# Batches 4 to 7: v as the standing operand in two column halves, kv transposed once a batch, z from sums on VectorE

## The chip, the cores and the metric

The kernel runs on one core of a Trainium2 chip. The metric is the device time of one execution in microseconds (us). Before the change the median of three runs is 1175.9 us (1174.65 to 1179.93). The engines have short names here, as in the profile: PE is TensorE (PEld its loads of the standing operand, "weights"), DVE is VectorE, ACT is ScalarE, POOL is GpSimd, SP is SyncE, which here issues DMAs. The suffix q means an engine's sequencer.

## What is computed

Random-feature attention over 8 batches, 8 heads, 576 rows and 64 columns a head, with 128 features, and behind it a gated feed-forward layer on 4608 rows:

```python
def phi(x):
    proj = np.einsum('bhsd,md->bhsm', x, omega)
    sq = np.sum(x * x, axis=-1, keepdims=True) / 2.0
    h = proj - sq
    h = h - np.max(h, axis=-1, keepdims=True)
    return np.exp(h) / np.sqrt(m)
q_p, k_p = (phi(q_s), phi(k_s))
kv = np.einsum('bhsm,bhsd->bhmd', k_p, v)
z = np.sum(k_p, axis=2)
num = np.einsum('bhsm,bhmd->bhsd', q_p, kv)
den = np.einsum('bhsm,bhm->bhs', q_p, z)[..., None] + 1e-06
...
silu = g * (1.0 / (1.0 + np.exp(-g)))
return (silu * val @ w_out).astype(np.float32)
```

`q_s` and `k_s` are q and k scaled; g and val are the attention's output (4608 x 512) times two 512 x 1536 matrices; `w_out` is 1536 x 512.

## The kernel before

The attention runs in 72 steps (`steps`, L124 to L127). Each step has two slots, and a slot is a group of 256 rows of a pair of heads, or the last 64 rows of all four pairs of a batch (a rest group, `None` in `kgroups` and `qgroups`). A batch has 9 groups of k and 9 of q. The first 6 steps (`AHEAD`) hold two k groups each, the next 60 one q group and one k group, the last 6 two q groups. So the k groups of batches 4 to 7 lie in steps 30 to 65, and the q groups of batch 4 begin at step 42.

What a group goes through is spread over several steps. `st_transpose` (L393) turns its rows (`pt`, `x`), `st_project` (L412) multiplies them with omega (`pp`; the two heads of a pair lie in two halves of the array's rows), `st_max` (L431) finds maxima on DVE, `st_exp` (L451) makes the features `ph` on ACT. For k, `k_accumulate` (L543) follows two steps later (`KLAG`): the features `ph` stand in the array (128 x 128), and v with a column of ones, 65 columns, moves. So kv comes out with features as rows, and z as its 65th column. The accumulator `kvacc` holds two pairs of heads (`a2` is 0 or 1); when it is complete, `kv_finalize` (L472) copies it to `kvr`.

For q there are two ways. Batches 0 to 3 (`b < BPOOL`) are multiplied with kv and z at once (`q_mult`, L589), divided on DVE, and turned in `q_out` by a transpose (L635). For batches 4 to 7 the denominator is made ahead: `q_den` (L504) multiplies the features with z on POOL, which needs z in all 128 partitions (`zt`), and sums on DVE (`dj`); `q_norm` scales the features, `q_transpose` turns them (`ptq`, L585, copied to `qt`), and `q_out` (L627) multiplies with kv standing, one head in each half of the array's columns (`xt`, L642). To spread z, `kv_finalize` turns it on PE (`zp`, L481), ACT copies it (`zs`), a DMA writes it to DRAM (`zd`), and at the step of the batch's first q group `load_z` reads it back into all partitions.

PSUM is scarce. `ps_att` (tag "b"), `ps_tr` (tag "t") and the accumulators of kv (tag "kv") have one bank each. `ptq` of the first q group of a step lies in `ps_att`, and so do `zp`, and `xt` of a step's second q group.

Between these parts the layer's products run on the same PE: `g` and `v` at L678 and `o` at L687, each of 512 moving columns, later `a`, `c`, `d` at L912. How many of them a step takes is set ahead by a plan of costs (`course`, `give`); the order of the parts within a step is the list `GROUPED` from step 25 on. A scheduler of the framework makes the final order of each engine, and may move an instruction past others of its engine; `issue_after` and `behind_step` (L257) forbid some of that. Each engine executes its instructions in order. Where the output of a group is for tiles 3 to 8 it goes through a copy `xo` (L656) and a DMA to DRAM (`xs`).

At the start q, k and v are loaded by SP, except v of the first step and of the first rest group (`vrest`, four DMAs), which ACT issues (L387).

Of the kernel before, what the change touches and what calls it, by code (L numbers as in the profile page):

```python
# [23 lines left out]
def kernel(  # L24
# [11 lines left out]
    nc = tc.nc  # L36
# [57 lines left out]

    ident = const.tile([P, P], F32, name="ident")
    make_identity(nc, ident)

    def ps_att(name, shape):
        return ps_a.tile(shape, F32, name=name, tag="b")
# [30 lines left out]
    def slots(n, kind):  # L130

        if not 0 <= n < NS:
            return []
        return [(i, b, g, (kgroups if kd == "k" else qgroups)[g]) for i, (kd, b, g) in enumerate(steps[n]) if kd == kind]

    def pairs_of(gr):
        return [(2 * c, 2 * c + 1) for c in range(CH)] if gr is None else [gr[:1]] * CH
# [240 lines left out]
    def load_v(n):  # L378
        for i, b, g, gr in slots(n, "k"):
            rest = gr is None  # L380
            ts = (vtile, vrest)[rest]
            t = ts[nv[rest] % len(ts)]
            nv[rest] += 1
            assert t not in busy, "v's tile is still needed"
            busy.append(t)
            vrows[b, g] = t
            load_group(t, v, b, gr, True, nc.scalar if n == 0 or n < AHEAD and gr is None else nc.sync)  # L387

    box = {}
    sts = {}  # L390


    def st_transpose(n):  # L393
        if n >= NS:
            return
        nat = nats.pop(n)
        pt = ps_tr(f"pt_{n}", [P, 2, G])
        for i in range(2):
            for c in range(CH):
                nc.tensor.transpose(  # L400
                    pt[:, i, c * P : (c + 1) * P], nat[:, i, c].rearrange("p h d -> p (h d)"), ident
                )
        x = att.tile([P, 2, G], F32, name=f"x_{n}", tag="x")

        st = att.tile([P, 4, 2, CH, 2], F32, name=f"st_{n}", tag="st", bufs=6)
        sq = att.tile([P, 2, CH, 2, D], F32, name=f"sq_{n}", tag="sq")
        nc.gpsimd.tensor_tensor(sq, nat, nat, op=ALU.mult)  # L407
        nc.scalar.copy(x, pt)  # L408
        sts[n] = x, st, sq
        return True  # L410

# [60 lines left out]
    def kv_finalize(b, a2):  # L472
        acc = kvacc.pop((b, a2))
        raw = att.tile([P, 4, VW], F32, name=f"kvr{b}_{a2}", tag="kvr", bufs=4)
        nc.scalar.copy(raw, acc)
        for j in range(2):
            kvst[b, 2 * a2 + j] = raw[:, 2 * j : 2 * j + 2, :]
        if b >= BPOOL:

            zp = ps_att(f"zp{b}_{a2}", [4, P])  # L480
            nc.tensor.transpose(zp, raw[:, :, D], ident)  # L481
            zs = att.tile([4, P], F32, name=f"zs{b}_{a2}", tag="zs")
            nc.scalar.copy(zs, zp)
            zd = dram.tile([4, P], F32, name=f"zd{b}_{a2}", tag="zd", bufs=4)
            nc.sync.dma_start(zd, zs)
            zds[b, a2] = zd

    zds = {}
    zbc = {}

    def load_z(n):

        for _, b, g, gr in slots(n, "q"):
            if g == 0 and b >= BPOOL:
                zt = att.tile([P, 2, 4, M], F32, name=f"zt{b}", tag="zt")
                for a2 in range(2):
                    nc.sync.dma_start(
                        zt[:, a2], zds.pop((b, a2)).rearrange("(o h) m -> o h m", o=1).broadcast_to([P, 4, M])
                    )
                    zbc[b, a2] = zt[:, a2]  # L500

    dns = {}

# [39 lines left out]
    def k_accumulate(n, half):  # L543

        n -= KLAG
        ks = [(b, g, gr, c) for _, b, g, gr in slots(n, "k") for c in range(CH)]
        for b, g, gr, c in ks[half * len(ks) // 2 : (half + 1) * len(ks) // 2]:
            ph, vt = box["k", b, g], vrows[b, g]
            if c == CH - 1:
                busy.remove(vt)  # L550
                del box["k", b, g]
            for j, pr in enumerate(pairs_of(gr)[c]):
                a2 = pr // 2
                first = (b, a2) not in kvacc
                if first:
                    kvacc[b, a2] = ps_k.tile([P, 4, VW], F32, name=f"kvacc{b}_{a2}", tag="kv")
                acc = kvacc[b, a2]
                done.setdefault((b, a2), []).append(pr)
                last = LAST[pr] == (g, c)
                for hh in range(2):  # L560
                    nc.tensor.matmul(  # L561
                        acc[:, 2 * (pr % 2) + hh, :],
                        ph[:, c, hh * M : (hh + 1) * M],
                        vt[:, 2 * c + j if gr is None else c, hh, :],
                        start=first and hh == 0,
                        stop=last,
                        skip_group_check=True,
                    )
                if len(done[b, a2]) == NACC:
                    kv_finalize(b, a2)  # L570
        return bool(slots(n, "k"))

    qts = {}
    xns = {}
# [52 lines left out]
    def q_out(n):  # L627
        n -= OLAG
        for i, b, g, gr in slots(n, "q"):
            po = (ps_att if n + OLAG < EARLY or i else ps_tr)(f"xt{b}_{g}", [P, G])  # L630
            first = column(b, gr)
            if b < BPOOL:
                xn = xns.pop((b, g))
                for c in range(CH):
                    nc.tensor.transpose(po[:, c * P : (c + 1) * P], xn[:, c].rearrange("p h d -> p (h d)"), ident)  # L635
            else:
                qt = qts.pop((b, g))

                segs = [(pr, pr * RES, RES) for pr in range(NPAIR)] if gr is None else [(gr[0], 0, G)]
                for pr, o, w in segs:  # L640
                    for hh in range(2):
                        nc.tensor.matmul(  # L642
                            po[hh * D : (hh + 1) * D, o : o + w], kvst[b, pr][:, hh, 0:D], qt[:, hh, o : o + w],
                            start=True, stop=True, skip_group_check=True,
                        )
            j, o = tile_of(first)
            if gr is None:
                parts_ = [(po.rearrange("d (r c) -> d r c", c=RES), slice(0, NPAIR), j, o, RES)]
            else:
                cut = min(TILES[j][1] - o, G)  # L650
                parts_ = [(po[:, 0:cut], gr[0], j, o, cut)]
                if cut < G:
                    parts_.append((po[:, cut:G], gr[0], j + 1, 0, G - cut))
            for src, pr, j, o, w in parts_:
                if j in x_dram:
                    xo = att.tile(list(src.shape), F32, name=f"xo{b}_{g}_{j}", tag="xo", bufs=3)  # L656
                    nc.scalar.copy(xo, src)
                    nc.sync.dma_start(x_dram[j][:, pr, o : o + w], xo)
                    continue
                if j not in xt:  # L660
                    xt[j] = [xres.tile([P, NPAIR, T], F32R, name=f"x{e}{j}", tag=f"x{e}") for e in "hl"]
                hi, lo = (t[:, pr, o : o + w] for t in xt[j])
                nc.scalar.copy(hi, src)
                nc.vector.tensor_tensor(lo, src, hi.bitcast(F32), op=ALU.subtract)
            if gr is None or gr[0] == NPAIR - 1:
                cols_done[0] = first + (RES if gr is None else G)
        return bool(slots(n, "q"))
# [383 lines left out]
    def give(us):  # L1051
# [28 lines left out]
    )  # L1080
    GROUPED = (
        q_out,
        st_project,
        q_transpose,
        lambda n: k_accumulate(n, 0),
        lambda n: k_accumulate(n, 1),
        st_max,
        st_exp,
        q_den,
        lambda n: st_transpose(n + 1),  # L1090
# [18 lines left out]
    for n in range(NN):  # L1109
        load(n + LA)  # L1110
        load_v(n + LAV)
        if n == FIRST_RAW:
            load_raw(0)
        want = OPS * np.interp(clock[n + 1], [clock[m] for m, _ in marks], [x for _, x in marks])
        order = CLOSE if n < EARLY else GROUPED
        left = len(order) if n < EARLY else order.count(SHARE)
        for what in order:
            if what is not SHARE:
                what(n)
            if n < EARLY or what is SHARE:  # L1120
                due = course[n + 1] - given[0] - debt[0]
                if due > 0:
                    give(due / left)
                for _ in range(int(np.ceil((want - ticks[0]) / left))):
                    tick()
                left -= 1
        load_z(n)
    late.close()
    for name, pool in (
        ("win", tc.tile_pool(name="win", bufs=1)),  # L1130
# [38 lines left out]
```

## Time and profile before

| | |
|---|---|
| median of 3 runs | 1175.9 us (1174.65 to 1179.93) |
| the profiled execution | 1172.79 us, span 1171.0 us |
| granted clock of TensorE | 0.999 |
| DVE, ACT, POOL busy | 630.0, 678.3, 569.1 us |
| HBM read, written | 87.10 MB, 25.18 MB |
| attention (last of its products on PE) | to about 741 us of the span |

A row of the groups of instructions reads: line, engine, operation, output<-inputs, shapes, count, then busy time in us and the mean of one in ns, then the engine's idle time before it and what ended it. In a PE row `128*64 128x256` means a standing operand of 128 rows and 64 columns, and 256 columns moving. A row of the timeline reads: start in us, length in us, engine, line, operation, operands, count; like instructions that follow each other are one row. One float32 product of the program stands as two LDWEIGHTS and two MATMUL records (two passes); a transpose stands as one. The ends of matmuls are modelled and overlap the next start, so the time of a row of products is read here from its start to the start of the next row.

### The profile page before, as it was taken

Reading aid. Unit: us, or ns where it says so; the run is one execution under the profiler, and the core shown is the slowest. Engines: PE = TensorE matmul, PEld = TensorE weight load, DVE = VectorE, ACT = ScalarE, POOL = GpSimd, SP = SyncE. Lnnn points to the kernel's source line nnn. Section 1 sums busy time; section 2 is a strip of 40 time slices with the busy share of each in tenths; the row PEclk is TensorE's granted clock in tenths of the full one; section 3 lists DMA queues with packets and bytes.
Section 4 is the critical chain, followed back from the end, with each engine's and each line's share of the span. In section 5 each row is a group of like instructions: output and inputs, shape, how many; then the busy total and the mean of one; then the engine's idle time right before and its main releaser. Section 6 shows DMA issues by size and latency. Waiting matters only on the chain.

```text
span 1171.0 us, 18724 instructions
## 1 busy us (share of the span) xinstructions
PE 1149.5 (98%) x6705; PEld 951.7 (81%) x6705; DVE 630.0 (54%) x1159; ACT 678.3 (58%) x1499; POOL 569.1 (49%) x500
## 2 busy tenths in 40 slices
PE   7999999999999999999999999999999999999998
PEld 6998778888888888888888777878778888888886
DVE  5876667535466554334332552462566666456654
ACT  5898887775666665665466665334544445444441
POOL 3342353433365465554445765244655543455551
PEclk9999999999999999999999999999999999999999
DMA  7654355643454442443232212424311112211103
GB/s 168 155 147 116 108 168 164 177 127 111 127 155 131 125 118 70 120 105 82 64 80 73 60 46 81 127 81 123 93 53 47 48 53 54 72 55 54 45 19 73
DMA packets 174109, 113.52 MB, mean 97 GB/s; under 512 B 125856, under 2 KB 144320, under 8 KB 174016
## 3 DMA queue, kind: packets, MB, share of 16 engines
q1 hardware_dynamic: 172096, 111.86, 35.2%
q8 instruction: 53, 0.87, 0.3%
q10 hardware_dynamic: 1920, 0.46, 0.2%
q14 instruction: 40, 0.33, 0.1%
HBM read 87.10 MB, written 25.18 MB: 96 GB/s over the span
## 4 chain that ended last, share of the span: by engine, by line
PE 73%; DVE 5%; ACT 3%; DMA 2%; issue 2%; POOL 1%; SPq 1%; POOLq 0%; DVEq 0%; ACTq 0%
PE o L687 22%; PE g L678 11%; PE a L912 10%; PE v L678 10%; PE c L912 5%; PE pp L423 3%; PE d L912 3%; PE kvacc L561 2%; PE ptq L585 2%; PE xt L642 2%; PE pt L400 1%; DMA wraw<-wscr 1%; ACT ph L459 1%; DMA first_b<-xs 1%; POOL wlo L252 1%
## 5 line engine op out<-in xcount | busy, mean ns | idle before, releaser
L407 POOL TENSOR_TENSOR sq<-nat 128x512 f32<-128x512 f32 x72 | 75.9, 1055 | 199.3 <-DVE st L437 157.3
L716 DVE TENSOR_TENSOR acc<-o,acc 128x512 f32<-128x512 f32 x140 | 95.6, 687 | 128.6 <-PE o L687 128.2
L459 ACT ACTIVATE ph<-pp,st 128x128 f32<-128x128 f32 x576 | 157.0, 387 | 6.4 <-DVE st L447 5.7
L444 DVE TENSOR_REDUCE st<-pp 128x4 f32<-128x512 f32 x144 | 93.3, 686 | 95.7 <-PE pp L423 95.4
L252 POOL TENSOR_TENSOR wlo<-wraw,whi 128x512 fp32r<-128x512 f32 x76 | 103.1, 1366 | 64.0 <-ACT whi L251 62.4
L678 PE MATMUL g<-xh,whi 128*128 128x512 f32 x240 | 96.3, 401 | 0.9 <-DVE sl L771 0.9
L678 PE MATMUL v<-xh,whi 128*128 128x512 f32 x240 | 95.6, 398 | 0.5 <-DVE acc L716 0.5
L687 PE MATMUL o<-whi,hh 128*128 128x512 f32 x240 | 95.9, 400 | 0.0
L423 PE MATMUL pp<-omT,x 64*128 64x128 f32 x1152 | 90.9, 289 | 4.6 <-ACT x L408 4.6
L687 PE MATMUL o<-whi,hl 128*128 128x512 f32 x240 | 93.8, 391 | 0.9 <-POOL hl L775 0.9
L775 POOL TENSOR_TENSOR hl<-sl,hh 128x512 fp32r<-128x512 f32 x60 | 77.9, 1302 | 33.7 <-ACT hh L774 33.5
L678 PE MATMUL g<-xl,whi 128*128 128x512 f32 x240 | 94.0, 392 | 0.0
L678 PE MATMUL g<-xh,wlo 128*128 128x512 f32 x240 | 94.0, 392 | 0.0
L678 PE MATMUL v<-xh,wlo 128*128 128x512 f32 x240 | 93.9, 391 | 0.0
L687 PE MATMUL o<-wlo,hh 128*128 128x512 f32 x240 | 93.9, 391 | 0.0
L678 PE MATMUL v<-xl,whi 128*128 128x512 f32 x240 | 93.6, 390 | 0.0
L423 PEld LDWEIGHTS pp<-omT,x 64*128 64x128 f32 x1152 | 73.9, 189 | 21.8 <-issue 11.6
L899 POOL TENSOR_TENSOR wlo<-wspare,whi 128x512 fp32r<-128x512 f32 (+1 forms) x40 | 40.5, 1032 | 75.0 <-ACT whi L898 68.6
L771 DVE TENSOR_TENSOR sl<-v,sl 128x512 f32<-128x512 f32 x60 | 40.9, 685 | 60.8 <-PE v L678 60.8
L251 ACT CAST whi<-wraw 128x512 fp32r<-128x512 f32 x76 | 46.6, 629 | 42.1 <-PE v L678 24.4
L525 DVE TENSOR_REDUCE dj<-jk 128x4 f32<-128x512 f32 x36 | 24.6, 685 | 83.8 <-POOL jk L521 69.1
L774 ACT CAST hh<-sl 128x512 fp32r<-128x512 f32 x60 | 37.5, 626 | 51.9 <-DVE sl L771 51.7
(257 smaller groups left out, 2938.4 us busy)
## 6 DMA issues: line engine op xcount, KB each, us to landing
wraw<-wscr SPq DMA_DIRECT2D x80, 256.0 KB, 2.7
wspare<-wscr SPq DMA_DIRECT2D x40, 256.0 KB, 2.7
wscr<-wc SPq DMA_DIRECT2D x36, 256.0 KB, 2.2
out_dram<-acc SPq DMA_DIRECT2D x72, 128.0 KB, 2.3
nat<-in_k_dram SPq DMA_DIRECT2D x64, 128.0 KB, 3.1
nat<-in_q_dram SPq DMA_DIRECT2D x64, 128.0 KB, 3.1
v<-in_v_dram SPq DMA_DIRECT2D x62, 128.0 KB, 3.0
st<-in_moe_w_gate_dram SPq DMA_DIRECT2D x12, 512.0 KB, 3.9
```

Of the source, the lines that this page charges most:

```text
L251: nc.scalar.copy(hi, raw)
L252: nc.gpsimd.tensor_tensor(lo, raw, hi.bitcast(F32), op=ALU.subtract)
L407: nc.gpsimd.tensor_tensor(sq, nat, nat, op=ALU.mult)
L423: nc.tensor.matmul(pp[hh][:, i, c, :], x[r, i, c * P : (c + 1) * P], omT[r], start=True, stop=True)
L444: nc.vector.tensor_reduce(st[:, 1, :, :, hh], pp[hh], axis=AX.X, op=ALU.max, negate=True)
L459: step_end["s"] = nc.scalar.activation(ph[:, c, hh * M : (hh + 1) * M], pp[hh][:, i, c, :], AF.Exp, bias=st[:, 3, i, c, hh : hh + 1], scal ...
L678: nc.tensor.matmul(ps, a_[:, ws], b_[:, c, :], start=n == 0, stop=n == 3 * NC - 1)
L687: nc.tensor.matmul(ps, a_[:, ts_], b_, start=first and n == 0, stop=last and n == 2)
L716: nc.vector.tensor_tensor(a_, po, a_, op=ALU.add)
L771: nc.vector.tensor_tensor(h, pv, h, op=ALU.mult)
L775: nc.gpsimd.tensor_tensor(hl, h, hh.bitcast(F32), op=ALU.subtract)
L912: nc.tensor.matmul(ps, a_[:, w_], b_[:, c, :], start=start and c == 0 and m == 0, stop=c == CH - 1 and m == 2, skip_group_check=True,)
```

## The change

For the k groups of batches 4 to 7, `k_columns` takes the place of `k_accumulate`. Now v (64 columns) stands and `ph` (128 columns) moves; the two heads of a pair take the two halves of the array's columns, and the accumulator `kvt` of a whole batch (four pairs, one bank) holds kv with v's columns as rows. It is called right behind `q_out`. When a batch is complete ACT copies the accumulator, and in the next step `kv_turn` turns it with four transposes into `ps_att` and copies it to `kvr` in two pieces.

z no longer comes from a column of ones. `z_sum` adds the features of each k group on DVE into `zsums` (128 x 512, two a batch), one step after they are made and behind `st_max`: one add of 128 x 256 for the first group of pairs 0 and 1, two for every other group, four of 64 x 256 for a rest group. `z_spread` multiplies a matrix of ones with `zsums` (512 moving columns, in `ps_att`), which sums over the partitions and leaves z in all of them at once; ACT copies it to `zt`. The turn `zp`, the copy `zs`, the write `zd` and the broadcast load `zt` are gone, and with them `load_z`.

Two smaller edits: `xo` has two buffers in place of three, and the loads of v that are traced behind the first copy of `x` stay behind it in ACT's queue (this concerns the four `vrest` DMAs that ACT issues).

```diff
+    ones = const.tile([P, P], F32, name="ones")
+    nc.vector.memset(ones, 1.0)
...
-            load_group(t, v, b, gr, True, nc.scalar if n == 0 or n < AHEAD and gr is None else nc.sync)
+            by_act = n == 0 or n < AHEAD and gr is None
+            with tc.issue_after(first_copy[0].ins) if first_copy else ExitStack():
+                load_group(t, v, b, gr, True, nc.scalar if by_act else nc.sync)
...
-        nc.scalar.copy(x, pt)
+        copied = nc.scalar.copy(x, pt)
+        if not first_copy:
+            first_copy.append(copied)
...
-        if b >= BPOOL:
-
-            zp = ps_att(f"zp{b}_{a2}", [4, P])
-            nc.tensor.transpose(zp, raw[:, :, D], ident)
-            zs = att.tile([4, P], F32, name=f"zs{b}_{a2}", tag="zs")
-            nc.scalar.copy(zs, zp)
-            zd = dram.tile([4, P], F32, name=f"zd{b}_{a2}", tag="zd", bufs=4)
-            nc.sync.dma_start(zd, zs)
-            zds[b, a2] = zd
...
+    def z_sum(n):
+
+        for _, b, g, gr in slots(n - 1, "k"):
...
+            with behind_step():
+                if gr is None:
+                    for c in range(CH):
+                        for j in range(2):
+                            rows = slice(j * RES, (j + 1) * RES)
+                            to = zsums[b, c][rows, j]
+                            nc.vector.tensor_tensor(to, ph[rows, c], to, op=ALU.add)
+                    continue
+                pr, r = gr
+                to = zsums[b, pr // 2][:, pr % 2]
+                if pr < 2 and r == 0:
+                    nc.vector.tensor_tensor(to, ph[:, 0], ph[:, 1], op=ALU.add)
+                else:
+                    for c in range(CH):
+                        nc.vector.tensor_tensor(to, ph[:, c], to, op=ALU.add)
+
+    def z_spread(n):
+
+        for b, a2 in list(zsums):
+            if n != (qstep[b, 2] + JLAG if a2 else qstep[b, 0]):
+                continue
+            zp = ps_att(f"zp{b}_{a2}", [P, 4, M])
+            nc.tensor.matmul(
+                zp.rearrange("p h m -> p (h m)"), ones, zsums.pop((b, a2)).rearrange("p j m -> p (j m)"),
+                start=True, stop=True,
+            )
+            zbc[b, a2] = att.tile([P, 4, M], F32, name=f"zt{b}_{a2}", tag="zt", bufs=3)
+            nc.scalar.copy(zbc[b, a2], zp)
+
+    def k_columns(n):
+
+        for _, b, g, gr in slots(n - KLAG, "k"):
...
+            acc = kvacc[b]
+            for c in range(CH):
+                for j, pr in enumerate(pairs_of(gr)[c]):
+                    for hh in range(2):
+                        nc.tensor.matmul(
+                            acc[hh * D : (hh + 1) * D, pr, :],
+                            vt[:, 2 * c + j if gr is None else c, hh, 0:D],
+                            ph[:, c, hh * M : (hh + 1) * M],
...
+            if done[b] == 2 * NACC:
+                turned[b] = att.tile([P, NPAIR, M], F32, name=f"kvt{b}", tag="x")
+                nc.scalar.copy(turned[b], kvacc.pop(b))
+
+    def kv_turn(n):
+
+        b, o = divmod(n - (AHEAD - 1), NG)
...
+        pt = ps_att(f"kvp{b}", [P, 2, 4, D])
+        for pr in range(NPAIR):
+            nc.tensor.transpose(
+                pt[:, pr // 2, 2 * (pr % 2) : 2 * (pr % 2) + 2].rearrange("p h d -> p (h d)"), kt[:, pr], ident
+            )
+        for a2 in range(2):
+            raw = att.tile([P, 4, VW], F32, name=f"kvr{b}_{a2}", tag="kvr", bufs=4)
+            nc.scalar.copy(raw[:, :, 0:D], pt[:, a2])
...
-                    xo = att.tile(list(src.shape), F32, name=f"xo{b}_{g}_{j}", tag="xo", bufs=3)
+                    xo = att.tile(list(src.shape), F32, name=f"xo{b}_{g}_{j}", tag="xo", bufs=2)
...
     GROUPED = (
         q_out,
+        k_columns,
         st_project,
         q_transpose,
         lambda n: k_accumulate(n, 0),
         lambda n: k_accumulate(n, 1),
+        kv_turn,
+        z_spread,
         st_max,
+        z_sum,
         st_exp,
         q_den,
         lambda n: st_transpose(n + 1),
...
-        load_z(n)
```

More of the change, by code (lines that the diff above doesn't have):

```diff
@@ L386, in load_v @@
             vrows[b, g] = t
-            load_group(t, v, b, gr, True, nc.scalar if n == 0 or n < AHEAD and gr is None else nc.sync)
+            by_act = n == 0 or n < AHEAD and gr is None
+            with tc.issue_after(first_copy[0].ins) if first_copy else ExitStack():
+                load_group(t, v, b, gr, True, nc.scalar if by_act else nc.sync)
     box = {}
     sts = {}
+    first_copy = []
     def st_transpose(n):
@@ L477, in kv_finalize @@
             kvst[b, 2 * a2 + j] = raw[:, 2 * j : 2 * j + 2, :]
-        if b >= BPOOL:
-            zp = ps_att(f"zp{b}_{a2}", [4, P])
-            nc.tensor.transpose(zp, raw[:, :, D], ident)
-            zs = att.tile([4, P], F32, name=f"zs{b}_{a2}", tag="zs")
-            nc.scalar.copy(zs, zp)
-            zd = dram.tile([4, P], F32, name=f"zd{b}_{a2}", tag="zd", bufs=4)
-            nc.sync.dma_start(zd, zs)
-            zds[b, a2] = zd
-    zds = {}
-    zbc = {}
[L491 to L500, printed above, removed]
+    zbc = {}
@@ new lines @@
+    zsums = {}
+    qstep = {(b, g): n for n in range(NS) for _, b, g, _ in slots(n, "q")}
+    turned = {}
+    def z_sum(n):
+        for _, b, g, gr in slots(n - 1, "k"):
+            if b < BPOOL:
+                continue
+            ph = box["k", b, g]
+            if gr is None or gr == (0, 0):
+                a2 = 0 if gr else 1
+                zsums[b, a2] = att.tile([P, 2, 2 * M], F32, name=f"zs{b}_{a2}", tag="zs")
+                if a2:
+                    nc.gpsimd.memset(zsums[b, a2], 0.0)
+            with behind_step():
[13 more added lines that the diff above has]
+                        nc.vector.tensor_tensor(to, ph[:, c], to, op=ALU.add)
@@ new lines, in z_spread @@
+    def z_spread(n):
+        for b, a2 in list(zsums):
+            if n != (qstep[b, 2] + JLAG if a2 else qstep[b, 0]):
+                continue
+            zp = ps_att(f"zp{b}_{a2}", [P, 4, M])
[5 more added lines that the diff above has]
+            nc.scalar.copy(zbc[b, a2], zp)
@@ new lines, in k_columns @@
+    def k_columns(n):
+        for _, b, g, gr in slots(n - KLAG, "k"):
+            if b < BPOOL:
+                continue
+            ph, vt = box.pop(("k", b, g)), vrows[b, g]
+            busy.remove(vt)
+            if b not in kvacc:
+                kvacc[b] = ps_k.tile([P, NPAIR, M], F32, name=f"kvt{b}", tag="kv")
+                done[b] = 0
+            acc = kvacc[b]
[6 more added lines that the diff above has]
+                            ph[:, c, hh * M : (hh + 1) * M],
+                            start=done[b] == 0,
+                            stop=LAST[pr] == (g, c),
+                            skip_group_check=True,
+                        )
+                    done[b] += 1
+            if done[b] == 2 * NACC:
+                turned[b] = att.tile([P, NPAIR, M], F32, name=f"kvt{b}", tag="x")
+                nc.scalar.copy(turned[b], kvacc.pop(b))
@@ new lines, in kv_turn @@
+    def kv_turn(n):
+        b, o = divmod(n - (AHEAD - 1), NG)
+        if o or b not in turned:
+            return
+        kt = turned.pop(b)
+        pt = ps_att(f"kvp{b}", [P, 2, 4, D])
+        for pr in range(NPAIR):
+            nc.tensor.transpose(
+                pt[:, pr // 2, 2 * (pr % 2) : 2 * (pr % 2) + 2].rearrange("p h d -> p (h d)"), kt[:, pr], ident
+            )
+        for a2 in range(2):
+            raw = att.tile([P, 4, VW], F32, name=f"kvr{b}_{a2}", tag="kvr", bufs=4)
+            nc.scalar.copy(raw[:, :, 0:D], pt[:, a2])
+            for j in range(2):
+                kvst[b, 2 * a2 + j] = raw[:, 2 * j : 2 * j + 2, :]
@@ L545, in k_accumulate @@
         n -= KLAG
-        ks = [(b, g, gr, c) for _, b, g, gr in slots(n, "k") for c in range(CH)]
+        ks = [(b, g, gr, c) for _, b, g, gr in slots(n, "k") for c in range(CH) if b < BPOOL]
         for b, g, gr, c in ks[half * len(ks) // 2 : (half + 1) * len(ks) // 2]:
@@ L570, in k_accumulate @@
                     kv_finalize(b, a2)
-        return bool(slots(n, "k"))
+        return bool(ks)
     qts = {}
```

## The prediction, made before the changed kernel was run

> **What bounds the kernel now.** I read the page first (busy shares, the chain that ended last), then the stretch that the change touches with its busy times, then the timeline of PE within single steps.
>
> ```profile
> span 1171.0 us, 18724 instructions
> PE 1149.5 (98%) x6705; PEld 951.7 (81%) x6705; DVE 630.0 (54%) x1159; ACT 678.3 (58%) x1499; POOL 569.1 (49%) x500
> PE 73%; DVE 5%; ACT 3%; DMA 2%; issue 2%; POOL 1%; SPq 1%; POOLq 0%; DVEq 0%; ACTq 0%
> ...
> 180.00:665.00 485.00, 482.52 (x2967) 396.39 (x2967) 227.54 (x461) 303.15 (x674) 244.08 (x213) 1.00 0.41 112
> ...
> PEld zp L481 <- ACT kvr L475: 2.3, 8, 0.4
> PEld o L687 <- DVE acc L716: 0.6, 2, 0.3
> PEld g L678 <- DVE sl L771: 0.4, 1, 0.4
> ```
>
> The fourth row is the stretch 180 to 665 us, in which k of batches 4 to 7 is accumulated: PE is busy 482.5 of 485 us at a granted clock of 1.00, PEld 396.4, DVE 227.5 (47%), ACT 303.2, POOL 244.1. PE is the bound there, and behind this stretch the layer's products go on without a break in PE; so time taken off PE here should come off the end one for one, as long as no wait takes its place. The last rows are waits of 150 to 745 us: 2.3 us of PEld's go to `zp`, and DVE holds it up for 0.6 and 0.4 us.
>
> **How much a product costs** I read from starts to starts.
>
> ```profile
> 507.25 0.39 PE L678 MATMUL v<-xh,wlo 128*128 128x512 f32 x1
> 507.57 0.65 PE L642 MATMUL xt<-qt,kvr 128*64 128x256 f32 x4
> 508.16 1.16 PE L423 MATMUL pp<-omT,x 64*128 64x128 f32 x16
> 509.25 0.66 PE L585 MATMUL ptq<-ident,ph 128*128 128x128 f32 x4
> 509.74 1.00 PE L561 MATMUL kvacc<-v,ph 128*128 128x65 f32 x8
> 510.58 0.61 PE L400 MATMUL pt<-ident,nat 128*128 128x128 f32 x4
> 510.94 0.48 PE L678 MATMUL v<-xh,whi 128*128 128x512 f32 x1
> ...
> 677.93 1.08 PE L642 MATMUL xt<-qt,kvr 128*64 128x256 f32 x8
> 678.94 1.16 PE L423 MATMUL pp<-omT,x 64*128 64x128 f32 x16
> ...
> 689.74 1.12 PE L642 MATMUL xt<-qt,kvr 128*64 128x64 f32 x20
> 690.79 0.38 PE L423 MATMUL pp<-omT,x 64*128 64x128 f32 x2
> ```
>
> A k group's eight records take 509.74 to 510.58, 0.84 us. The form that takes their place, 64 columns standing in two column halves, is in the trace as `xt`. Four records with 256 moving columns take 507.57 to 508.16, 0.59 us; eight take 1.01. So four more records cost 0.42. The simple reading is that the two column halves run at once, two pairs of 0.21 us. Entering and leaving the form costs 0.59 - 0.42 = 0.17 us. Twenty records (4 of 256 columns, 16 of 64) take 1.05, so eight pairs of 64 columns take 0.46, 0.058 each. The line through both ends is (0.21 - 0.058) / 192 = 0.79 ns a column with 0.007 us left over; at 128 columns a pair takes 0.11 us. (Read as four records one by one, the same rows give half of that for each record, and the same sum.)
>
> **The parts of the change, against the profiled execution.**
>
> Removed, products of k: 320 records, 40 rows like 509.74 (36 groups, four of them rest groups with two rows): 40 x 0.84 = 33.6 us.
>
> Added, the same in column halves: 160 pairs x 0.11 = 17.6 us. Bounds: 160 x 0.058 = 9.3 and 160 x 0.21 = 33.6, by the 64 and 256 column rows; I keep 17.6, since 128 lies on the line between them.
>
> Added, changes of form: where `q_out` has column halves already, `k_columns` stands behind it in the same form and enters nothing. In steps 32 to 44 (k of batch 4 on, before batch 4's first q reaches `q_out`) it is a full transpose, and 13 x 0.17 = 2.2 us are added.
>
> ```profile
> 235.42 0.38 PE L635 MATMUL xt<-ident,xn 128*128 128x128 f32 x2
> ...
> 237.31 1.00 PE L561 MATMUL kvacc<-vrest,ph 128*128 128x65 f32 x8
> 238.26 0.66 PE L400 MATMUL pt<-ident,nat 128*128 128x128 f32 x4
> 239.03 0.27 PE L481 MATMUL zp<-ident,kvr 128*4 128x128 f32 x1
> 239.13 1.00 PE L561 MATMUL kvacc<-vrest,ph 128*128 128x65 f32 x8
> ...
> 664.82 1.09 PE L585 MATMUL ptq<-ident,ph 128*128 128x128 f32 x8
> 665.67 0.48 PE L687 MATMUL o<-whi,hh 128*128 128x512 f32 x1
> ...
> 666.68 0.61 PE L400 MATMUL pt<-ident,nat 128*128 128x128 f32 x4
> ```
>
> Removed, the turn of z: eight times 0.10 (239.03 to 239.13) and the wait of 2.3 us in all: 3.1 us. Its ACT copies and 16 small DMAs on SP go too; nothing waits for them in time (z is used steps later), so they are worth nothing.
>
> Added, z by ones: eight products of 512 moving columns, two passes each. No row has that form in float32; at 0.79 ns a column a pass takes 0.41, and 8 x 0.82 = 6.6, with a first load I take 6.8 us. Bounds: 8 x 0.45 = 3.6, were a pass as quick as the layer's products (27 of them in 6.15 us, 0.228 each), and 8 x 1.09 = 8.7 by the longest row of its neighbours (`pp`, 16 records). The float32 row with two passes is the nearer.
>
> ```profile
> 496.05 6.15 PE o L687 x27
> ```
>
> Added, the turn of kv: four times four transposes, 0.36 (510.58 to 510.94) to 0.49 us (509.25 to 509.74): 1.7 us.
>
> Sum on PE: -33.6 + 17.6 + 2.2 - 3.1 + 6.8 + 1.7 = **-8.4 us**.
>
> New waits on PE: `kvp` and `zp` take the bank that `ptq` has just filled, so they wait for ACT's copy `qt`, and behind them in PE's queue stand the transposes for the next step and the layer's products. The bound is 12 x about 0.6 us (a copy) = 7 us; the other end is nothing, since the planner fills such waits: at 665.67 four products `o` stand between `ptq` and a `pt` that waits for a bank, and at 238.26 `pt` stands ahead of `zp`, though the program calls it later. I take 0.7 us.
>
> New work of DVE: 56 adds of 128x256 and 16 of 64x256.
>
> ```profile
> L880 DVE TENSOR_TENSOR s<-wspare,wspare x20: 414/422/1521, 810.6 to 1125.2; 128x256 f32<-128x256 f32 x20
> L525 DVE TENSOR_REDUCE dj<-jk 128x4 f32<-128x512 f32 x36 | 24.6, 685 | 83.8 <-POOL jk L521 69.1 <-POOL jk L517 14.8
> ```
>
> Such an add from SBUF takes 0.42 at the median and 1.52 at most: 72 x 0.42 = 30 us over 36 steps. They stand behind `st_max` and ahead of `dj`, before which DVE idles 83.8 us in 36 steps, 2.3 a step, waiting for POOL; 0.84 us a step fits in, and I take nothing. If that cover is gone the price is a rival below. ACT's larger copies (some 6 us in 485 with 180 idle) and POOL's four memsets hide as well.
>
> `xo` with two buffers: only steps with two q groups write three or four of them in a row, where a group is cut by a tile's end (three such steps).
>
> ```profile
> 705.00 0.32 ACT L657 COPY xo<-xt 128x192 f32<-128x192 f32 x1 [1.15 <-DMA xs<-xo]
> ...
> xs<-xo SPq DMA_DIRECT2D x30, 128.0 KB, 2.4
> ```
>
> Even three buffers made ACT wait 1.15 us once. With two the third copy waits for the first DMA (2.4 us); behind ACT stand `qt` and the layer's splits, behind the bank PE's next `ptq`. From nothing to 2 x 2.4 = 4.8 us; I take 1.2, since PE has the layer's products to go on with.
>
> The start: four `vrest` DMAs on ACT move behind the first `x`.
>
> ```profile
> 3.30 3.40 ACTq L365 DMA_DIRECT2D vrest<-in_v_dram  x4
> 6.73 1.28 ACT L337 ACT_TABLE_LOAD   x1 [6.73 <-DMA vrest<-in_v_dram]
> 8.20 0.58 ACT L408 COPY x<-pt 128x512 f32<-128x512 f32 x1
> ...
> 20.45 1.04 POOL L407 TENSOR_TENSOR sq<-nat 128x512 f32<-128x512 f32 x1 [3.22 <-DMA nat<-in_k_dram]
> 23.66 1.04 POOL L407 TENSOR_TENSOR sq<-nat 128x512 f32<-128x512 f32 x1 [2.18 <-DMA nat<-in_k_dram]
> ```
>
> The table load and `x` behind them could come up to 3.4 us sooner. But at 20.45 and 23.66 the squares wait for rows of k to land, so what is gained at 8 us is lost again by then unless the loads come sooner too, and the four issues then stand in ACT's queue before the exponentials. From -3.4 to +1; I take -0.5, nearer to the rows at 20 us.
>
> In all -8.4 + 0.7 + 1.2 - 0.5 = **-7.0 us**: 1165.8 against the profiled execution's 1172.8 (span 1171.0 and 1.8 around it). That execution was 3.1 us quicker than the median of the three runs, 1175.9, so I forecast **1169 us**, 0.6% below the median. About 0.5% (5.9 us) is what a measurement of this kernel can tell from no change.
>
> **The rivals.**
>
> *The gain is eaten by banks and buffers.* If half to most of the bounds for the shared bank (7) and `xo` (4.8) are paid instead of 1.9, 4 to 7 us are lost again: 1173 to 1176, say 1174. For it: both resources are single and tight. Against: the planner's filling.
>
> *Everything is hidden and the start pays in full*: -8.4 - 3.4 = -11.8, 1164.
>
> *The load of v stands in line.* If the array took the weights of a half only after the matmul before, each pair would cost a load more; the 64 column row bounds a load at 0.058, 160 x 0.058 = 9.3, so +2.3, 1178. Against: the line through the 64 and 256 column rows leaves only 0.007 us for anything that doesn't grow with the columns. The Trainium skill ("TensorE: Matmul & The Clock Gate", Part 3, what overlaps and what doesn't) says that a weight load overlaps a running matmul only where the row groups differ, and two column halves share their rows; by that rule this rival is what happens. The trace's `xt` rows disagree with the rule.
>
> *The halves don't run at once* with `ph` moving (each record takes 0.11), so the change doesn't do what it says: 17.6 us more, +10.6, 1187. Against: the same form as `xt`, in another order of the same program.
>
> *Slower: DVE becomes late.* Place: the adds of `z_sum` between `st_max` and the layer's products, whose PSUM banks DVE empties (L716, L771). Price: 0.42 us for each add that PE comes to wait for; one in each of 36 steps gives 15 us, +8, 1184; both at POOL-slowed lengths far more. It decides from 0.2 us a step (7.0 / 36) on. For it: PE waits for exactly these operations already, and adds up to 1.52 us occur. Against: those waits are 1.0 us in all, and DVE is idle 53% of the stretch.
>
> **How the numbers follow.** Chances: forecast 0.43 (its own range 1166 to 1171), eaten 0.26, larger gain 0.15, loads in line 0.05, halves one by one 0.03, DVE late 0.08. Over 0.5% faster (below 1170.0): most of the forecast and the larger gain, 0.52; slower: DVE and the halves and a little of the loads in line, 0.13; the rest, 0.35, within 0.5%. The range from 1163 (the larger gain and one us) to 1179 (loads in line) leaves out DVE, the halves, and tails of the others.
>
> **What would show it.** `kvt` rows of eight records taking 0.44 us to the next row confirm the halves, 0.9 refutes them, 0.67 shows loads in line. The product with ones should take 0.85 us. Waits of PE for `qt` before `kvp` or `zp`, for DVE before `g` or `o`, and of ACT for `xs` show the three ways to lose. The first `x` should move from 8.20 to about 5.5 us, and the squares at 20.45 and 23.66 by less than 1 us. Wrong I'd be above all if the planner placed the new products badly, which no row of before can show.

## The result and the profile after

The change makes the kernel slower: the median is 1184.0 us of 14 runs (1177.1 to 1187.2) against 1176.3 us of before, ratio 1.0060 with a 95% interval of 1.0047 to 1.0072, that is 7 us more where 7 us less were forecast. In all ratios here three slow executions are left out, one of start_alone (1911 us) and two of xo_three (6453 us). The profiled execution after the change has a span of 1185.4 us, 14.4 more than that of before. First its page and its waits of PE between 150 and 770 us:

```profile
span 1185.4 us, 18852 instructions
PE 1155.6 (97%) x6729; PEld 948.6 (80%) x6729; DVE 660.9 (56%) x1232; ACT 681.4 (57%) x1503; POOL 573.9 (48%) x504
PE 71%; DVE 4%; ACT 3%; DMA 3%; issue 3%; POOL 2%; SPq 0%; POOLq 0%; DVEq 0%; ACTq 0%
...
PE pt L405 <- ACT xo L730: 3.7, 4, 2.1
PE zp L524 <- ACT qt L660: 2.3, 2, 1.9
PE ptq L658 <- ACT xo L730: 1.3, 3, 0.6
```

PE is busier by 6 us although the products of k take some 12 us less (worked out below), and it now waits for ACT's copies out of shared banks, which in before it hardly did. (Lines differ from before: `zp` is now the product with ones, L524; `xo` L730; `qt` L660; `pt` L405.)

The time of the copy `x` of each step, read from both traces, shows where the 14.4 us come about:

```
copy x of step       4     30     42     44     48     68     71    end
before (us)       20.9  163.0  311.5  338.8  392.4  655.4  697.0  1171.0
after - before    +7.4   +8.2   +6.0  +10.3  +13.1  +10.1  +13.8   +14.4
```

8 us arise before step 12. They aren't put down to the change: the start varies from profile to profile, as the experiments and the last section show. From step 30 to 42, and from 48 to 68, the kernel gains 0.18 and 0.15 us a step, near the forecast's 7.0 / 36 = 0.19; it loses at steps 42 to 48 and behind 68. The timeline of PE and ACT at the first loss:

```profile
327.26 1.16 PE L430 MATMUL pp<-omT,x 64*128 64x128 f32 x16
328.35 0.66 PE L658 MATMUL ptq<-ident,ph 128*128 128x128 f32 x4
328.84 0.60 PE L405 MATMUL pt<-ident,nat 128*128 128x128 f32 x4
329.20 0.48 PE L760 MATMUL o<-whi,hh 128*128 128x512 f32 x1
329.51 0.40 PE L760 MATMUL o<-wlo,hh 128*128 128x512 f32 x1
331.77 1.75 PE L524 MATMUL zp<-zs,ones 128*128 128x512 f32 x2 [1.86 <-ACT qt L660]
```

```profile
330.62 0.62 ACT L253 CAST whi<-wraw 128x512 fp32r<-128x512 f32 x1 [3.36 <-DMA wraw<-wscr]
331.14 0.58 ACT L660 COPY qt<-ptq 128x512 f32<-128x512 f32 x1
```

`zp` must wait until `qt` has emptied the bank that `ptq` filled. `ptq` was done at 329, but in ACT's queue a cast of weights stood before `qt`, and that waited 3.36 us for a DMA. The planner had put two products `o` into the gap, and the gap became 1.86 us longer. The second loss is of the same kind, four steps later, but at a bank that the change doesn't touch: `pt` waits until `xo` has emptied the bank that `xt` filled.

```profile
384.92 0.65 PE L715 MATMUL xt<-qt,kvr 128*64 128x256 f32 x4
385.40 0.61 PE L545 MATMUL kvt<-ph,v 128*64 128x128 f32 x8
385.94 1.16 PE L430 MATMUL pp<-omT,x 64*128 64x128 f32 x16
387.03 0.66 PE L658 MATMUL ptq<-ident,ph 128*128 128x128 f32 x4
389.76 0.77 PE L405 MATMUL pt<-ident,nat 128*128 128x128 f32 x4 [2.07 <-ACT xo L730]
390.18 0.77 PE L751 MATMUL g<-xh,whi 128*128 128x512 f32 x1
390.75 0.63 PE L751 MATMUL g<-xl,whi 128*128 128x512 f32 x1
391.18 0.63 PE L751 MATMUL g<-xh,wlo 128*128 128x512 f32 x1
```

Behind both waits the clock of TensorE falls back to half. Products of 512 columns start every 0.43 us (390.75, 391.18) instead of every 0.23, and the busy times by stretch give the granted clock, third from the end of a row:

```profile
160.00:331.00 171.00, 165.40 (x1083) 136.00 (x1081) 100.22 (x213) 120.07 (x268) 68.69 (x60) 1.00 0.50 145
331.00:336.00 5.00, 4.23 (x10) 2.74 (x11) 1.52 (x4) 4.97 (x13) 2.26 (x2) 0.66 0.90 236
336.00:390.00 54.00, 51.92 (x331) 41.58 (x330) 35.73 (x70) 29.68 (x64) 30.62 (x26) 1.00 0.39 114
390.00:394.00 4.00, 4.00 (x14) 3.23 (x13) 3.93 (x6) 2.13 (x7) 3.00 (x3) 0.57 0.38 102
```

0.66 over 5 us and 0.57 over 4 us are each 1.7 us lost, (1 - 0.66) x 5 and (1 - 0.57) x 4. So the two waits cost 1.9 + 2.1 + 2 x 1.7 = 7.4 us. The clock falls in most executions, but not in all: of the 14 runs ten have a granted clock of 0.997 or less, with a median of 1184.4 us, and four have 0.999 or 1.0, with a median of 1179.3.

### The profile page after: what moved, and what is told of

Read it like the earlier page. It is cut to its first block, busy times and chain, and to the rows that moved or that the text cites. A ratio compares the mean times of both kernels' runs of the same rounds, so it can differ in the third digit from the quotient of the medians.

```text
span 1185.4 us, 18852 instructions
## 1 busy us (share of the span) xinstructions
PE 1155.6 (97%) x6729; PEld 948.6 (80%) x6729; DVE 660.9 (56%) x1232; ACT 681.4 (57%) x1503; POOL 573.9 (48%) x504
## 4 chain that ended last, share of the span: by engine, by line
PE 71%; DVE 4%; ACT 3%; DMA 3%; issue 3%; POOL 2%; SPq 0%; POOLq 0%; DVEq 0%; ACTq 0%
PE o L760 21%; PE g L751 11%; PE a L985 10%; PE v L751 10%; PE c L985 5%; PE pp L430 3%; PE d L985 3%; PE ptq L658 2%; PE pt L405 1%; PE kvt L545 1%; PE xt L715 1%; DMA wraw<-wscr 1%; DMA xs<-xo 1%; PE po L675 1%; DMA first_b<-xs 1%
## 5 line engine op out<-in xcount | busy, mean ns | idle before, releaser
L430 PE MATMUL pp<-omT,x 64*128 64x128 f32 x1152 | 93.6, 295 | 5.2 <-ACT x L413 5.2
L430 PEld LDWEIGHTS pp<-omT,x 64*128 64x128 f32 x1152 | 76.4, 195 | 18.3 <-issue 7.0
L660 ACT COPY qt<-ptq 128x512 f32<-128x512 f32 x72 | 42.0, 592 | 41.1 <-PE ptq L658 40.7
```

The source lines that it names most:

```text
L430: nc.tensor.matmul(pp[hh][:, i, c, :], x[r, i, c * P : (c + 1) * P], omT[r], start=True, stop=True)
L660: nc.scalar.copy(qts[b, g], pt)
```

## The experiments

All ratios are of runs against runs of the kernel before; each experiment stands against before on the same chip, in five rounds; since three chips were used, versions are compared by their ratios. "Step 30 on" is the span of one profile against before's, less what was lost up to step 30; that takes out the start.

| run | ratio, 95% interval | step 30 on, us |
|---|---|---|
| the change | 1.0060, 1.0047 to 1.0072 | +6.2 |
| start_undone | 1.0064, 1.0044 to 1.0084 | +4.4 |
| start_alone | 1.0007, 0.9990 to 1.0025 | -0.6 |
| z_alone | 1.0101, 1.0083 to 1.0118 | +10.9 |
| xo_alone | 1.0028, 1.0014 to 1.0042 | +1.6 |
| early_spread | 0.9995, 0.9981 to 1.0010 | +1.8 |
| late_own_bank | 0.9996, 0.9978 to 1.0015 | -0.2 |
| early_own_bank | 0.9983, 0.9966 to 0.9999 | -2.6 |
| xo_three | 1.0008, 0.9991 to 1.0025 | +1.8 |
| all_three | 0.9980, 0.9964 to 0.9996 | -3.4 |
| z_best | 1.0053, 1.0034 to 1.0073 | +7.9 |
| halves_no_z | 0.9882, 0.9860 to 0.9905 | -13.3 |
| z_split | 0.9965, 0.9949 to 0.9980 | -6.6 |

**Is it the start?** My first reading of the two traces was that the four `vrest` loads had cost the 8 us.

```diff
-            with tc.issue_after(first_copy[0].ins) if first_copy else ExitStack():
+            with ExitStack():
                 load_group(t, v, b, gr, True, nc.scalar if by_act else nc.sync)
```

> The changed kernel with the edit of the start undone: the four vrest loads go where the scheduler puts them, all else stays changed. Theory A (the start costs the loss: the fifth x comes 7.4 us later in the profile after, and the distance stays at 8.1 us for 30 steps): about 8 us less than the changed kernel, so 1176 against its median of 1184, within 0.3% of the kernel before, with the fifth x back at 21 us. Rival B (the loss comes from the products and waits in the middle and only shows at the start by chance): under 3 us less, 1181 or more.

The kernel before with these lines of the change alone (issue_after kept, nothing else changed):

> The kernel before with the edit of the start alone. Theory A: 7 to 8 us slower than before, 1184, with the fifth x at about 28 us and TensorE's clock at half for some 15 us longer. Rival B: within 2 us of before.

Theory A fell twice: 1184.5 us without the edit, 1177.0 with it alone. The fifth `x` comes at 27.3 us in start_undone and at 23.4 in start_alone: the start varies, with or without the edit. The edit itself is worth between -1 and +3 us. The table bears this out: the ratio, in us, and the column without the start agree within 3.1 us in every row, on either side, so no version has a start that is 8 us later as a rule.

**The parts.** All batches with the features standing, z by sums:

```diff
-        ks = [... for c in range(CH) if b < BPOOL]
+        ks = [... for c in range(CH)]
         q_out,
-        k_columns,
...
-        kv_turn,
         z_spread,
```

> As start_undone, but all batches keep the features standing (no column halves, no turn of kv); z by DVE's sums and the product with ones, xo with two buffers. If the column halves are worth what the step rows say (33.6 - 17.6 - 2.2 - 1.7 = 12 us), this is 12 us slower than start_undone, about 1188. If their gain is eaten elsewhere, it is within 4 us of start_undone.

1186.9 us: 2.4 above start_undone by the medians, 4.4 by the ratios, so at the edge of the second case; z_alone has no fall of the clock, start_undone has two. The late wait of `zp` lies in both (1.7 us in z_alone), so the sums bring it without the halves; and what the halves are worth doesn't show while start_undone pays for its waits and falls of the clock.

```diff
-                    xo = att.tile(..., tag="xo", bufs=3)
+                    xo = att.tile(..., tag="xo", bufs=2)
```

> The kernel before with two xo buffers in place of three. Theory (prediction's term): 1.2 us slower, 1177.5. Rival (waits of ACT for xs add up as in the profile after, 6.3 us in 4 waits against 1.1 in one): 4 to 6 us slower, 1180 to 1182.

3.3 us (1.6 to 4.9), between the two: the waits of ACT for `xs` grow from 1.1 us in one to 6.3 in four.

**Which wait?** In the trace after the change DVE's adds pause from 292 to 333 us, and the reason stands in the row:

```profile
292.07 0.41 DVE L516 TENSOR_TENSOR zs<-ph,zs 128x256 f32<-128x256 f32 x1
333.56 0.76 DVE L513 TENSOR_TENSOR zs<-ph 128x256 f32<-128x256 f32 x2 [2.83 <-PE zp L524]
334.24 0.88 DVE L516 TENSOR_TENSOR zs<-ph,zs 128x256 f32<-128x256 f32 x2
```

A batch has two tiles of sums and there are two buffers; the next batch's first add comes at step 9b + 4, while `z_spread` reads this batch's first tile only at step 9b + 6. So the adds of three steps wait for `zp`. I had not seen this in the diff. Theory C made it the cause, rival D the shared bank.

```diff
-            if n != (qstep[b, 2] + JLAG if a2 else qstep[b, 0]):
+            if n != ((qstep[b, 1] if b < B - 1 else qstep[b, 2] + JLAG) if a2 else qstep[b, 0] - 3):
```

> As start_undone, but z is spread earlier: the first half of a batch's z three steps before its first q group, the second half at its second q group (batch 7: as it was), so that a batch's sums are read before the next batch needs their two buffers. Theory C (DVE's adds for the next batch wait for the product with ones, 2.8 us in one piece, then come in a heap, and PE is late behind DVE and ACT from step 42 to 47): 4 to 7 us less than start_undone, 1178 to 1180, DVE's wait for zp gone. Rival D (the shared bank is the cause: zp waits for ACT's copy qt, the clock falls back for 3.4 us): under 2 us less.

And on top of it the other bank:

```diff
-            zp = ps_att(f"zp{b}_{a2}", [P, 4, M])
+            zp = ps_moe(f"zp{b}_{a2}", [P, 4, M])
...
-        pt = ps_att(f"kvp{b}", [P, 2, 4, D])
+        pt = ps_moe(f"kvp{b}", [P, 2, 4, D])
```

> As early_spread, and z's product and kv's turn use a bank of the layer's products instead of the one that ptq has filled. Theory C: within 1.5 us of early_spread. Rival D: 3 to 6 us less than early_spread, the waits of PE for qt before zp and kvp (6.2 us of PEld in the profile after) gone.

The bank without the earlier spreading:

> As start_undone with z's product and kv's turn in a bank of the layer's products; z is spread as late as in the change. Theory C (late spreading and two buffers of sums): the gain of early_spread isn't there, 1180 or more, DVE still waits for zp. Rival D (the bank alone): 1174 to 1177, as early_own_bank.

Spreading early brings 0.69% (8 us), more than C asked; the bank alone brings 0.68%, where C asked for nothing; both together 0.81%, 1.4 us less than early_spread, which is what C asked. So neither is the cause by itself. What both remove is one wait, `zp` behind a late `qt`: with early spreading `zp` comes at steps where `qt` isn't late, with the own bank it doesn't depend on it. Two of the waits of PE in late_own_bank, then in early_spread:

```profile
PE pt L405 <- ACT xo L730: 4.4, 5, 2.1
PE ptq L658 <- ACT xo L730: 1.3, 3, 0.7
```

```profile
PE ptq L658 <- ACT xo L730: 3.3, 3, 2.7
PE pt L405 <- ACT xo L730: 1.7, 5, 0.5
```

No `zp` in either. The second wait, 2.1 us of `pt` for `xo` at 386 us, with its fall of the clock, stays in late_own_bank and is gone in early_spread (which has a new one, 2.7 us of `ptq` at 725 us, and 1.1 us of `o` for DVE's `acc`). The trace after the change shows how it hangs on the late spreading, on POOL, DVE and ACT:

```profile
375.04 0.53 POOL L501 MEMSET zs<- 128x512 f32 x1 [8.05 <-PE zp L524]
383.44 1.04 POOL L610 TENSOR_TENSOR ph<-ph,dj 128x512 f32<-128x512 f32 x1 [2.50 <-DVE dj L600]
...
375.60 2.75 DVE L508 TENSOR_TENSOR zs<-ph,zs 64x256 f32<-64x256 f32 x2
378.38 2.85 DVE L516 TENSOR_TENSOR zs<-ph,zs 128x256 f32<-128x256 f32 x2
386.47 0.53 DVE L282 TENSOR_SCALAR wc<-wc 128x512 f32<-128x512 f32 x1 [2.47 <-ACT wc L279]
...
385.75 0.69 ACT L279 ACTIVATE wc<-st 128x512 f32<-128x512 f32 x1 [1.09 <-POOL wlo L254]
388.81 0.62 ACT L847 CAST hh<-sl 128x512 fp32r<-128x512 f32 x1 [1.87 <-DVE sl L844]
389.34 0.37 ACT L730 COPY xo<-xt 128x256 f32<-128x256 f32 x1
```

POOL stands for 8.05 us, since the tile of sums that it has to clear is only free when the batch's second `zp` is done. Then four adds come in a heap and take 1.4 us each instead of 0.42. Behind them DVE makes `dj`, for which POOL waits; then POOL's `wlo`, ACT's and DVE's `wc`, DVE's `sl`, and ACT's `hh` wait for one another, and `xo` stands behind `hh`. In the runs with early spreading POOL waits for no `zp` here, and no add takes over 0.43 us (0.9 in z_best). That this chain makes the whole of the wait is argued, not shown by a run of its own. z_alone has the same heap, 4.6 us from 370.2 on, but there the products `kvacc` stand between `ptq` and `pt`, and `pt` waits 0.46 us. What stays in both is `ptq` behind `xo` after 700 us.

**Three buffers for `xo`**, first in start_undone, then in early_own_bank; room for the third comes from `st`.

```diff
-        st = att.tile(..., tag="st", bufs=6)
+        st = att.tile(..., tag="st", bufs=3)
...
-                    xo = att.tile(..., tag="xo", bufs=2)
+                    xo = att.tile(..., tag="xo", bufs=3)
```

> As start_undone with three xo buffers again (room for it: st has three buffers instead of six, of which two are in use at a time). By xo_alone (0.28% slower) 3.3 us less than start_undone, 1181; if xo's waits only take the place of others, the same as start_undone. Steps 68 to 71 lose 0 instead of 3.6 us against before.

> As early_own_bank with three xo buffers. If the three causes add up and the start costs nothing: 1184 - 5 - 3 - 3.3 = 1172 to 1173, quicker than before by 3 us; with the whole sum of PE's terms 1168. If the gain of the column halves isn't there at all: 1176 or more.

xo_three gains 0.56% (6.6 us), more than `xo` costs alone, and all_three gains nothing measurable over early_own_bank. By the medians the fixes don't add. By the profiles xo_three gains 2.6 us from step 30 on, its waits of `zp` (1.5) and `pt` (2.1) stand, and the clock falls back once instead of twice. From step 68 to 71 it loses 2.6 us against before, where 0 was expected: `xo` isn't what costs most there. How often the clock falls back varies between executions, and the granted clocks of all runs put about 2 us of the 6.6 down to it (a mean of 0.9967 in start_undone, 0.9984 in xo_three). The rest stays open.

all_three is quicker than before by 0.2% (the interval ends just under 1), and 5 us short of the forecast sum. Where are they?

**Halves and z apart.** all_three without `z_sum` and `z_spread`: z of batches 4 to 7 is left out, a constant tile takes its place.

```diff
+    ztc = att.tile([P, 4, M], F32, name="ztc", bufs=1)
+    nc.gpsimd.memset(ztc, 1.0)
...
-        z_spread,
         st_max,
-        z_sum,
```

> As all_three, with z left out for batches 4 to 7: no sums on DVE, no product with ones, the features of q are multiplied with a constant. If z costs what PE's rows say (16 records, 7.2 us): 1168 against all_three's 1175. If DVE's adds hold PE up as well: 1165 or less. If PE's gain is lost whatever stands beside it: 1173 to 1175.

And all_three with the features standing, as in z_alone:

> As all_three (early spread, own bank, three xo buffers), with the features standing for all batches: no column halves, no turn of kv. If the halves are worth 34.0 - 21.7 + 2.3 - 1.7 = 13 us of PE, less about 2 for the refilled passes around them: 1186. Against before this is z's way alone: 4 us more on PE by its rows (7.2 for the product, 2.8 less for the turn and its wait), 1180; both can't be true, since all_three itself is 1175: the measured value says which of the two terms is smaller than its rows.

The column halves without any z are 1.18% quicker than before (13.9 us), which has its own z to pay for; z by sums costs all_three 0.98% of it again (11.5 us, 9.9 by the profiles from step 30 on). Its rows on PE hold 7: a product takes 289.12 to 289.98, 0.86 us, eight times:

```profile
288.63 0.66 PE L658 MATMUL ptq<-ident,ph 128*128 128x128 f32 x4
289.12 1.02 PE L524 MATMUL zp<-zs,ones 128*128 128x512 f32 x2
289.98 0.60 PE L405 MATMUL pt<-ident,nat 128*128 128x128 f32 x4
```

z_best is 0.53% slower than before (4 to 9 us), so z by sums is dearer than z by a column of ones and a DMA, even at its best place. By z_best the halves are worth 0.73% (8.6 us, 11.3 by the profiles) when z stands beside them.

**A cheaper product.** The sums are split in a rounded part (fp32r) and its remainder, and the product with ones becomes two of one pass.

```diff
+            hi = att.tile([P, 4 * M], F32R, name=f"zh{b}_{a2}", tag="x")
+            lo = att.tile([P, 4 * M], F32R, name=f"zl{b}_{a2}", tag="jx")
+            nc.scalar.copy(hi, zs)
+            nc.vector.tensor_tensor(lo, zs, hi.bitcast(F32), op=ALU.subtract)
...
-            nc.tensor.matmul(..., ones, zsums.pop((b, a2))..., start=True, stop=True)
+            nc.tensor.matmul(zp.rearrange("p h m -> p (h m)"), ones, hi, start=True, stop=False)
+            nc.tensor.matmul(zp.rearrange("p h m -> p (h m)"), ones, lo, start=False, stop=True)
```

> As all_three, with the sums of z split in a rounded part and its remainder, so that the product with ones is two products of one pass each instead of two float32 passes; the copy on ACT and the subtraction on DVE are added at the step's beginning. By the rows (a layer's product of 512 columns 0.228 us, a float32 pass 0.45): 8 x 0.44 = 3.5 us less than all_three, ratio to before 0.995. If z's price beyond its PE rows (halves_no_z is 11.6 us quicker than all_three, the rows hold 7) comes from the work around the product, nothing is gained or it is slower: 0.998 or more.

0.9965: 4 us less than before, the quickest version with z in it. Against all_three it is 0.15% (1.8 us), and the intervals overlap; the expected 3.5 can't be told from half of it. In its trace the product takes 0.55 us in place of 0.86, so PE's rows hold 2.5 us. The split changes a second thing, too: the tile of sums is free as soon as it is split, and POOL, which in all_three waits 6.4 us for `zp` before it clears one, no longer does. Which of the two makes the gain wasn't separated.

## Why the prediction was wrong

The time of PE's products from the copy `x` of step 30 to that of step 71, each counted from its start to the next start, as worked out from the traces (`pp` and `po` are equal in all three; a wait counts to the row ahead of it):

```
us        kvacc    kvt    xt   kvp    zp    pt   ptq     g      o     v    all
before     35.6    0    20.8   0     0.6  17.5  20.8  126.6  128.6  127.0  534.0
after - b -34.0  +21.8  -2.3  +1.7  +4.5  -2.2  +4.2   +4.3   +6.1   +1.3   +5.6
all_three
 - before -34.0  +21.7  -2.3  +1.7  +6.7  -2.2  +2.4   -0.1   +1.5   +0.5   -4.1
```

**The sum on PE was right.** Products of k removed 33.6, measured 34.0. Halves and changes of form 17.6 + 2.2 = 19.8, measured 21.7 - 2.3 = 19.4: behind `xt` the eight `kvt` records add 0.43 us (384.92 to 385.94 is 1.02, where `xt` alone took 0.59), forecast 0.44. The turn of kv 1.7, measured 1.7. z's product 6.8 less 3.1, measured in all_three 6.7 (the product less the old turn's 0.6) - 2.2; in the change itself the layer's products stand around z's, and part of its price counts to `g`, `o` and `v`. In all_three these six terms come to -8.4, the forecast to a tenth; that it is a tenth is luck, since z came out 0.8 dearer and the two others 0.4 cheaper each.

**The step that failed is the price of the new waits on PE**, 0.7 for the shared bank and 1.2 for `xo`. I bounded the first by "12 x about 0.6 us (a copy)". But what PE waits for is not the copy, it is all that stands before the copy in ACT's queue: 1.9 and 2.1 us in single waits, because casts stood there that themselves waited for a DMA or for DVE. "The planner fills such waits" was true and didn't help: it filled what it foresaw (two `o` at 329.20) and its orders are fixed. And each long wait had a second price that I had left out, 1.7 us of half clock. Together 7.4 us.

A third price stood nowhere in the sum: the halves themselves make `pt` wait for `xo`. In before `kvacc` stood between `ptq` and `pt` and gave ACT time for `xo`; now `kvt` stands ahead of `pp`, and from `xt` to `pt` PE needs 1.02 + 1.09 + 0.49 = 2.6 us in place of 0.59 + 1.09 + 0.49 + 0.84 = 3.0. So part of what the halves save is waited for again. PE's waits of `pt` for `xo` come to 1.7 to 4.4 us in each of the nine runs with halves and to at most 1.0 in the five without, and the column `ptq`, +4.2, has 2.1 of it beside the long wait.

The 3.7 us behind step 68 (+10.1 to +13.8) are for the greater part no wait: 2.0 us are the last turn of kv and z's last two products (terms of the sum, where no products of k are left to save), and 1.0 is lost there by xo_alone as well, so the 1.2 for `xo` was about right in this stretch.

From step 30 to 71 the whole is 5.6 + 8.4 = 14 us beside a forecast of 1.9: 7.4 for the two long waits and their clock, 2.1 for the other waits of `pt`, 1.0 for `xo`; some 3.5 us in small pieces weren't traced one by one (among them the loads of `zp` that wait for `qt`, 5.0 us in 8 on PEld, where PE itself shows 2.3 in 2). The rival that the gain is eaten by banks and buffers had the kind of loss right and half its size; it priced neither the clock nor the bank of `pt`.

**z** was forecast at +6.8 - 3.1 = 3.7 net; z_best measures 4 to 9 us. The wait of 2.3 us that I took off with `zp` goes only when the halves come too: in z_best `pt` loses 0.5 us, in all_three 2.2, since the other half of a rest group waits for the same copy `kvr` of the single accumulator bank. And halves_no_z puts z's price beside the halves at 11.5 us, 4 us above its rows on PE; these 4 (3 by the profiles) were not traced to single waits.

**DVE** did not become the bound in the way of that rival: in the stretch PE waits for DVE's `acc` once in all_three (1.1 us) and not at all in the change. That its 1184 is the measured number is luck. But the adds weren't hidden as I argued either: the "I take nothing" counted DVE's idle time and not the two buffers, through which DVE and POOL had to wait for PE's `zp`; the heap that came of it leads, through POOL and ACT, to the second long wait.

**The start**: `x` moved from 8.2 to 6.2 us (forecast about 5.5), and the second `x` from 12.0 to 12.9, behind the four issues; the squares moved by -1.3 and +0.3 us, where less than 1 was forecast. Nothing measurable is left, against -0.5.

**Loads in line** fell: the row of `kvt` alone takes 0.54 us, between the 0.44 of the halves and the 0.67 of this rival, but `xt` ahead of it is 0.11 shorter, and in total the halves cost 19.4 us where loads in line would have made it 19.8 + 9.3 = 29.1. The Trainium skill's rule on this ("TensorE: Matmul & The Clock Gate", Part 3, what overlaps and what doesn't) isn't borne out by this form.

## What to carry to other kernels

A PE sum worked out from start to start in the trace held here, within 1 us for each term; a wait on a shared bank can't be priced by the copy that frees it, only by the queue before that copy, and each such wait may cost the clock as well. Products that are taken out of PE's queue may have been the time in which another engine emptied a bank. When an accumulated tile is read late, count its buffers against the step in which the next one begins. An operation that is moved from a DMA to the bound engine needs its full price there: here the cheaper product of k, with no z at all, was worth 14 us, and the new way to z took 11 of them.

## What was not expected of the hardware

The clock fell to half after waits of only 1.86 and 2.07 us, for 3.41 us each time. It did so behind all six waits of 1.86 to 2.09 us in the change, start_undone, late_own_bank and xo_three, not behind those of 1.48 to 1.69 us in xo_three, halves_no_z, z_split and z_alone, and not behind one of 2.70 us in early_spread (`ptq` at 725 us). So the length of the wait alone doesn't decide it. The Trainium skill ("TensorE: Matmul & The Clock Gate", Part 1) speaks of an idle window of about 3.4 us before the clock falls back; its length agrees with the 3.41 us, the idle time before it here is shorter.

The start varies with the moment at which the clock is first released: by 4 to 5 us between programs with the same code at the start (before and xo_alone, or early_spread and all_three), and by 8 us between before and the change. Eight products `kvacc` and sixteen `pp` of the same form, in the profile after, then in before:

```profile
17.69 1.91 PE L634 MATMUL kvacc<-v,ph 128*128 128x65 f32 x8
19.53 2.08 PE L430 MATMUL pp<-omT,x 64*128 64x128 f32 x16
```

```profile
14.83 1.06 PE L561 MATMUL kvacc<-v,ph 128*128 128x65 f32 x8
15.82 1.16 PE L423 MATMUL pp<-omT,x 64*128 64x128 f32 x16
```

The first record of the full clock stands at 12.5 us in before, at 17 to 18 us in start_alone, z_alone, early_spread and xo_three (3 us late at step 30), at 21.5 in xo_alone and 22.6 in early_own_bank (4.5 and 5.2 late) and at 27 to 28 us in the change, start_undone and all_three (7 to 8 late); about half of the delay is what is lost. In the change PE is busy for all of the 10 us from 18 to 28, and the clock is still at half. z_split has it at 12.6, but falls to half for 6.83 us at 46.7 and is 3.8 late. Why the moment differs was not found. One profile against another says nothing about a start here.
